# Attention beside a two-layer MLP and a routed MLP on one core: the second score product on 128 rows, and the high part of the weights cast on ScalarE throughout

## The chip, the core and the metric

The kernel runs on one core of a Trainium2 chip. The core has a matrix engine (TensorE, PE in the profile, with its weight loads as PEld), VectorE (DVE), ScalarE (ACT), GpSimd (POOL) and SyncE (SP), which here only issues transfers. Each engine works through its own instructions in the order in which the program lists them, and waits on semaphores for the others. The metric is the device time of one execution in microseconds, the median of the runs; lower is better.

## The reference

Four batches of eight heads, 576 tokens, 64 numbers a head. Queries and keys are rotated, their scores go through a softmax, and the weights multiply the values. The result, 2304 rows of 512, goes through a two-layer MLP with a leaky ReLU, and then through a second MLP whose weights are those of the best of eight experts, chosen row by row.

```python
def rotate(x):
    x1, x2 = (x[..., :half], x[..., half:])
    return np.concatenate([x1 * cos - x2 * sin, x1 * sin + x2 * cos], axis=-1)
scores = scale * np.matmul(rotate(q), rotate(k).transpose(0, 1, 3, 2))
attn = np.exp(scores - np.max(scores, axis=-1, keepdims=True))
x = np.matmul(attn / (np.sum(attn, axis=-1, keepdims=True) + 1e-09), v)
...
h = x @ w_in
y = np.maximum(0.01 * h, h) @ w_out
...
expert_idx = np.argmax(logits, axis=1)
for e in range(E):
    mask = expert_idx == e
    out[mask] = gate_w[mask, None] * (np.maximum(y[mask] @ w1[e], 0.0) @ w2[e])
```

## The kernel before, in words

**Numbers in two parts.** Queries, keys, values, weights of the softmax and rows of the MLP are each held as a high part in 16 bits and a low part (what the rounding left), so that products of 16-bit numbers add up to nearly 32-bit accuracy.

**Pairs and units.** Two heads form a pair g; there are 16 pairs. A pair has nine units: u = 0 to 7 are 128 queries of one head each, u = 8 is the last 64 queries of both heads. That makes 144 units.

**Preparing a pair** (`prep`, lines 372 to 478). The pair's queries and keys are rotated, scaled, and split into the tile `stg` [128 tokens, 5 slots, 5 blocks, 128]. Slots 0 and 1 hold the queries, one slot a head: head 0 as high | low, head 1 as low | high. Slots 2 and 3 hold each head's keys' high part twice side by side: ScalarE writes it once (line 421), VectorE copies it (line 469, 443 for the first pair). Slot 4 holds the low parts of both heads side by side. One transfer that transposes (line 474, 25 blocks of 128 by 128) turns `stg` into `stk`, where the numbers lie on the partitions: `stk[:, h]` has a head's query parts on its two halves, `stk[:, 2 + h]` the keys' high part on both halves, and `stk[:, 4]` the keys' low parts, one head a half.

**A unit's stages.** Scores (`a_scores`, line 494): for each half of the keys (288 columns) a first product over all 128 rows, line 502, gives (high + low of q) times high of k, and a second over the 64 rows of that head, line 503, adds high of q times low of k. That is four products a unit, eight for u = 8. Then the maximum on VectorE (line 510), the exponential E on ScalarE (line 515), the weights' high part (`a_hi`), their low part on VectorE (line 527), a transposing transfer of both to `PT` (line 531), the products with the values (line 548), and ScalarE's copy of the result (`xo`, line 558). `a_hi` runs on ScalarE (line 521) as long as some job that decodes the MLP's weights lives, and on VectorE (line 523) after that: 54 units and 90 units.

**The MLP's units.** A unit of the MLP is h (line 266, twelve products of 256 columns, or 24 of 128), ScalarE's scaled copy g (line 274), VectorE's leaky ReLU (line 278), ScalarE's cast gh (line 282), GpSimd's low part gl (line 286), and six products into acc (line 297). The PSUM tile that h is written to has one buffer, so the next h waits for the leaky ReLU of the last.

**What sets the order.** Everything is issued in a hand-written order (`step`, line 1002). Step i runs the exponential and the later stages of unit i - 1, the maximum of unit i, the value products of unit i - 4, the scores of unit i + 1, and at most one unit of the MLP. The stages within a step follow one of three strings; the third, once the MLP's weights are decoded, is `FESXfHsLGVKAshlC2x` (E exponential, X maximum, H the high part, L the low part and the transfer, S h, G g, K leaky ReLU, h gh, V values, C scores, 2 the products into acc). Side work (preparing pairs, finishing rows, routing, decoding weights) is cut into pieces; a piece is taken in a slot (`s`, `x`) when its step has come and the estimated budgets of the engines allow. After the last unit the rest of the MLP's units run alone, and then the experts.

Of the kernel before, what the change touches and what calls it, by code (L numbers as in the profile page):

```python
# [36 lines left out]
HI_ACT = 1  # L37
# [64 lines left out]
def attention_moe_kernel(ctx: ExitStack, tc: tile.TileContext, qkv, w_in, w_out, emb, tau, w1, w2,  # L102
# [269 lines left out]
    def prep(g):  # L372
# [37 lines left out]
        def stacks():  # L410
            stg = qkp.tile([128, 5, 5, 128], F16, name="stg")
            s2 = stg.rearrange("p s c x -> p (s c x)")
            qhi = s2[:, 0:1408].rearrange("p (h x) -> p h x", h=2)[:, :, 0:640].rearrange("p h (c x) -> p h c x", c=5)[:, :, :, 0:64]
            return (s2, qhi, stg[:, 2:4], [stg[:, 0, :, 64:128], stg[:, 1, :, 0:64]],
                    [stg[:, 4, :, 64 * h:64 * h + 64] for h in range(2)])
# [11 lines left out]
        if g == 0:  # L427
# [9 lines left out]
            s2, qhi, khd, qlo, klo = stacks()  # L437
# [3 lines left out]
            hi(khd[:, :, :, 0:64], 1)  # L441
            lo(qlo, 0, qhi)
            nc.vector.tensor_copy(out=khd[:, :, :, 64:128], in_=khd[:, :, :, 0:64])
            lo(klo, 1, khd[:, :, :, 0:64])
        else:
# [17 lines left out]
            s2, qhi, khd, qlo, klo = stacks()  # L463
            yield Piece(A=1.44)
            hi(qhi, 0)
            hi(khd[:, :, :, 0:64], 1)
            yield Piece(V=1.2)
            lo(qlo, 0, qhi)
            nc.vector.tensor_copy(out=khd[:, :, :, 64:128], in_=khd[:, :, :, 0:64])
            yield Piece(V=0.93)  # L470
            lo(klo, 1, khd[:, :, :, 0:64])
        yield Piece(at=i0 - 1)
        stk = stp.tile([128, 5, 640], F16, name="stk")
        nc.sync.dma_start_transpose(out=stk.rearrange("p s (c x) -> p (s c) x", c=5), in_=s2)
# [19 lines left out]
    def a_scores(g, u):  # L494
        stk = pairs[g][0]
        ps = psS.tile([128, 2, 512], F32, name="S")
        todo = [(u % 2, u // 2 * 128, 128, 0)] if u < 8 else [(0, 512, 64, 0), (1, 512, 64, 64)]
        for n in range(2):
            ks = slice(288 * n, 288 * n + 288)
            for h, c0, m, o in todo:  # L500
                hr = slice(64 * h, 64 * h + 64)
                nc.tensor.matmul(ps[o:o + m, n, 0:288], lhsT=stk[:, h, c0:c0 + m], rhs=stk[:, 2 + h, ks], start=True, stop=False)  # L502
                nc.tensor.matmul(ps[o:o + m, n, 0:288], lhsT=stk[hr, h, c0:c0 + m], rhs=stk[hr, 4, ks], start=False, stop=True)  # L503
        return ps
# [13 lines left out]
    def a_hi(e, i):  # L518
        p = pep.tile([128, 2 * S], F16, name="P", bufs=3)
        if i % (HI_ACT if M.unit else HI_A1) == 0 and any(z.live for z in wjobs):  # L520
# [776 lines left out]
```

## Time and profile before

| | us |
|---|---|
| median of 3 runs | 1069.04 |
| the three runs | 1068.91, 1069.04, 1073.39 |
| the profiled execution, its own time | 1070.07 |
| its span, first to last instruction | 1068.2 |
| TensorE busy, of the span | 956.1 (90%) |
| VectorE busy | 825.6 (77%) |
| ScalarE busy | 701.0 (66%) |
| GpSimd busy | 366.3 (34%) |

The span falls into four stages: up to about 183 us the MLP's weights are decoded beside the first 39 units; to about 262 us the decoding runs out while the MLP's units have begun; to 683 us the other units and the MLP's units share the step; after 683 us come the rest of the MLP and the experts. A row of the timeline has the start, the length, the engine, the line, output and inputs, and a count where like instructions are merged; in brackets stands the engine's idle time before it and what ended it. Ends of products are modelled, so the time from one product's start to the next one's start says more than a product's length.

### The profile page before, as it was taken

Reading aid. Unit: us, or ns where it says so; the run is one execution under the profiler, and the core shown is the slowest. Engines: PE = TensorE matmul, PEld = TensorE weight load, DVE = VectorE, ACT = ScalarE, POOL = GpSimd, SP = SyncE. Lnnn points to the kernel's source line nnn. Section 1 sums busy time; section 2 is a strip of 40 time slices with the busy share of each in tenths; the row PEclk is TensorE's granted clock in tenths of the full one; section 3 lists DMA queues with packets and bytes.
Section 4 is the critical chain, followed back from the end, with each engine's and each line's share of the span. In section 5 each row is a group of like instructions: output and inputs, shape, how many; then the busy total and the mean of one; then the engine's idle time right before and its main releaser. Section 6 shows DMA issues by size and latency. Waiting matters only on the chain. (4 is left out here: it accounts for less than half of the span.)

```text
span 1068.2 us, 19714 instructions
## 1 busy us (share of the span) xinstructions
PE 956.1 (90%) x6737; PEld 710.7 (67%) x6737; DVE 825.6 (77%) x1670; ACT 701.0 (66%) x1349; POOL 366.3 (34%) x414
## 2 busy tenths in 40 slices
PE   1667767888999999999999999999999899999996
PEld 1334334656666767677776677778877778888885
DVE  6999998887799764887988867313476999998992
ACT  6878878777646645556665544535345888888883
POOL 2244432534335432453444423322233362211111
PEclk9999999989999999999999999999999999999999
DMA  8988989875867873488678654201152111115190
GB/s 227 192 195 219 231 198 174 173 158 112 166 115 125 190 106 82 67 156 168 104 148 158 92 115 83 60 2 41 30 179 103 36 60 41 53 47 198 34 344 20
DMA packets 273611, 133.54 MB, mean 125 GB/s; under 512 B 244951, under 2 KB 253399, under 8 KB 273504
## 3 DMA queue, kind: packets, MB, share of 16 engines
q1 hardware_dynamic: 270304, 122.24, 52.6%
q0 software_dynamic: 3200, 9.97, 2.8%
q8 instruction: 55, 0.90, 0.3%
q14 instruction: 52, 0.43, 0.1%
HBM read 120.04 MB, written 10.49 MB: 122 GB/s over the span
## 5 line engine op out<-in xcount | busy, mean ns | idle before, releaser
L266 PE MATMUL h<-xT,wi 128*128 128x256 f16 (+1 forms) x1920 | 215.7, 264 | 20.5 <-DVE g L278 14.4
L286 POOL TENSOR_TENSOR gl<-g,gh 128x256 fp32r<-128x256 f32 x144 | 112.9, 784 | 329.7 <-ACT gh L282 304.2
L266 PEld LDWEIGHTS <-wi 128*128 128x128 f16 x1920 | 168.8, 99 | 65.0 <-issue 47.1
L297 PE MATMUL acc<-wo,gh 128*128 128x512 f32 x576 | 195.8, 421 | 0.0
L274 ACT ACTIVATE g<-h,uw 128x256 f32<-128x256 f32 (+1 forms) x160 | 70.1, 449 | 123.6 <-PE h L266 115.4
L278 DVE SCALAR_TENSOR_TENSOR g<-h,uw,g 128x256 f32<-128x256 f32 (+1 forms) x160 | 71.0, 452 | 102.4 <-ACT g L274 102.4
L282 ACT ACTIVATE gh<-g 128x256 fp32r<-128x256 f32 x144 | 60.1, 417 | 117.2 <-DVE g L278 116.5
L527 DVE SCALAR_TENSOR_TENSOR P<-E,P 128x576 f16<-128x576 f32 x144 | 119.8, 832 | 17.8 <-ACT P L521 15.4
L502 PE MATMUL S<-stk 128*128 128x288 f16 (+1 forms) x320 | 105.8, 331 | 29.1 <-ACT E L515 27.8
L548 PE MATMUL o<-v,PT 128*128 128x65 f16 (+3 forms) x1770 | 103.3, 215 | 30.1 <-ACT xo L558 14.7
L515 ACT ACTIVATE E<-S,amx,sc 128x576 f32<-128x576 f32 x144 | 117.8, 818 | 9.8 <-DVE E L510 9.5
L548 PEld LDWEIGHTS <-PT 128*128 128x128 f16 (+1 forms) x1770 | 92.3, 111 | 43.3 <-issue 25.2
L510 DVE TENSOR_SCALAR_CACHE_REDUCE E<-S,sc 128x576 f32<-128x576 f32 x144 | 116.4, 808 | 2.3 <-PE S L503 2.0
L297 PEld LDWEIGHTS acc<-wo,gh 128*128 128x128 f32 x576 | 98.2, 190 | 26.1 <-issue 0.5
L297 PE MATMUL acc<-wo,gl 128*128 128x512 f32 x288 | 114.8, 399 | 0.0
L503 PE MATMUL S<-stk 64*128 64x288 f16 (+1 forms) x320 | 106.2, 332 | 0.0
L503 PEld LDWEIGHTS <-stk 64*128 64x128 f16 (+1 forms) x320 | 31.3, 98 | 88.9 <-issue 67.8
L936 POOL DMA_INDIRECT out<-eo,idi x18 | 25.5, 1416 | 153.7 <-ACT eo L934 153.0
L390 POOL TENSOR_TENSOR t<-raw,tab 128x320 f32<-128x320 f32 x62 | 66.4, 1098 | 8.3 <-DMA raw<-in_qkv 8.3
L523 DVE TENSOR_SCALAR P<-E 128x576 f16<-128x576 f32 x90 | 52.8, 586 | 18.6 <-ACT E L515 16.9
L297 PEld LDWEIGHTS acc<-wo,gl 128*128 128x128 f32 x288 | 54.6, 190 | 13.6 <-POOL gl L286 0.9
L502 PEld LDWEIGHTS <-stk 128*128 128x128 f16 (+1 forms) x320 | 33.6, 105 | 33.6 <-issue 12.8
(237 smaller groups left out, 1883.2 us busy)
## 6 DMA issues: line engine op xcount, KB each, us to landing
rb<-in_w SPq DMA_DIRECT2D x78, 512.0 KB
ra<-in_w SPq DMA_DIRECT2D x76, 512.0 KB
raw<-in_qkv SPq DMA_DIRECT2D x15, 640.0 KB
raw<-in_w_in SPq DMA_DIRECT2D x16, 512.0 KB
raw<-in_w_out SPq DMA_DIRECT2D x16, 512.0 KB
raw<-in_qkv SPq DMA_DIRECT2D x18, 320.0 KB
x2s<-x SPq DMA_DIRECT2D x18, 256.0 KB
v<-v SPq DMA_DIRECT2D x16, 162.5 KB
```

Of the source, the lines that this page charges most:

```text
L266: nc.tensor.matmul(m.h[:, c0:c1], lhsT=wi[:, a, c, 128 * f:128 * f + 128], rhs=xT[j][:, 4 * b_ + c, 0:c1 - c0], start=(n == 0), stop=(n == ...
L274: nc.scalar.activation(out=m.g[:, c0:c1], in_=m.h[:, c0:c1], func=AF.Copy, scale=uw[:, f:f + 1])
L278: nc.vector.scalar_tensor_tensor(out=m.g[:, c0:c1], in0=m.h[:, c0:c1], scalar=uw01[:, f:f + 1], in1=m.g[:, c0:c1], op0=ALU.mult, op1=ALU.max)
L286: nc.gpsimd.tensor_tensor(out=m.gl, in0=m.g, in1=m.gh.bitcast(F32), op=ALU.subtract)
L297: nc.tensor.matmul(M.acc[t], lhsT=g_[:, tt], rhs=wo[:, a, f], start=(f == 0 and n == 0), stop=(f == NF - 1 and n == 2))
L390: eng.tensor_tensor(out=t2[t][:, :, :, o:o + 32], in0=raw[:, t, :, :, i:i + 32], in1=sn[:, :, o:o + 32].unsqueeze(1).to_broadcast([128, 2, ...
L502: nc.tensor.matmul(ps[o:o + m, n, 0:288], lhsT=stk[:, h, c0:c0 + m], rhs=stk[:, 2 + h, ks], start=True, stop=False)
L503: nc.tensor.matmul(ps[o:o + m, n, 0:288], lhsT=stk[hr, h, c0:c0 + m], rhs=stk[hr, 4, ks], start=False, stop=True)
L510: nc.vector.tensor_scalar(out=e.rearrange("p (a b) -> p a b", a=2), in0=ps[:, :, 0:288], scalar1=pairs[g][2][:, 1:2], scalar2=None, op0=AL ...
L515: nc.scalar.activation(out=e.rearrange("p (a b) -> p a b", a=2), in_=ps[:, :, 0:288], func=AF.Exp, scale=sc[:, 0:1], bias=mx)
L527: nc.vector.scalar_tensor_tensor(out=p[:, 576:1152], in0=e, scalar=P_UP, in1=p[:, 0:576], op0=ALU.mult, op1=ALU.subtract)
L548: nc.tensor.matmul(o[ob:ob + m, oc + z:oc + z + w], lhsT=pt[:, i, q0:q0 + m], rhs=v16[:, i, h, c:c + w], start=(n == 0), stop=(n == len(to ...
```

## The change

It has three edits. First, `stg` has four slots: two of queries, as before, one of the keys' high parts (both heads side by side) and one of their low parts. The key slots are transposed by themselves into a new tile `kt`, the query slots into `stk[:, 0:2]`, and four plain transfers of 64 partitions by 1280 numbers copy each head's keys, high and low, from its half of `kt` to both halves of `stk`. VectorE's copy of the high part is gone. Second, both score products of a unit run over all 128 rows: the second is now (high + low of q) times low of k, which adds the product of the two low parts. Third, `a_hi` goes to ScalarE in all 144 units. Besides, the on-chip memory set aside for descriptors of GpSimd's transfers shrinks from 16384 (the default) to 4096 bytes a partition.

```diff
         def stacks():
-            stg = qkp.tile([128, 5, 5, 128], F16, name="stg")
+            stg = qkp.tile([128, 4, 5, 128], F16, name="stg")
...
-            return (s2, qhi, stg[:, 2:4], [stg[:, 0, :, 64:128], stg[:, 1, :, 0:64]],
-                    [stg[:, 4, :, 64 * h:64 * h + 64] for h in range(2)])
+            return (s2, qhi, stg[:, 2].rearrange("p c (h x) -> p h c x", h=2), [stg[:, 0, :, 64:128], stg[:, 1, :, 0:64]],
+                    [stg[:, 3, :, 64 * h:64 * h + 64] for h in range(2)])
...
             yield Piece(A=1.44)
             hi(qhi, 0)
-            hi(khd[:, :, :, 0:64], 1)
-            yield Piece(V=1.2)
+            hi(khi, 1)
+            yield Piece(V=0.93)
+            lo(klo, 1, khi)
+            yield Piece(V=0.93)
             lo(qlo, 0, qhi)
-            nc.vector.tensor_copy(out=khd[:, :, :, 64:128], in_=khd[:, :, :, 0:64])
-            yield Piece(V=0.93)
-            lo(klo, 1, khd[:, :, :, 0:64])
+        yield Piece(at=i0 - 2)
+        kt = stp.tile([128, 2, 640], F16, name="kt", bufs=1)
+        nc.sync.dma_start_transpose(out=kt.rearrange("p s (c x) -> p (s c) x", c=5), in_=s2[:, 1280:2560])
         yield Piece(at=i0 - 1)
-        stk = stp.tile([128, 5, 640], F16, name="stk")
-        nc.sync.dma_start_transpose(out=stk.rearrange("p s (c x) -> p (s c) x", c=5), in_=s2)
+        stk = stp.tile([128, 6, 640], F16, name="stk")
+        nc.sync.dma_start_transpose(out=stk[:, 0:2].rearrange("p s (c x) -> p (s c) x", c=5), in_=s2[:, 0:1280])
+        for h in range(2):
+            for z in range(2):
+                nc.sync.dma_start(out=stk[64 * z:64 * z + 64, 2 + 2 * h:4 + 2 * h], in_=kt[64 * h:64 * h + 64])
...
-                hr = slice(64 * h, 64 * h + 64)
-                nc.tensor.matmul(ps[o:o + m, n, 0:288], lhsT=stk[:, h, c0:c0 + m], rhs=stk[:, 2 + h, ks], start=True, stop=False)
-                nc.tensor.matmul(ps[o:o + m, n, 0:288], lhsT=stk[hr, h, c0:c0 + m], rhs=stk[hr, 4, ks], start=False, stop=True)
+                for a in range(2):
+                    nc.tensor.matmul(ps[o:o + m, n, 0:288], lhsT=stk[:, h, c0:c0 + m], rhs=stk[:, 2 + 2 * h + a, ks], start=(a == 0), stop=(a == 1))
...
-        if i % (HI_ACT if M.unit else HI_A1) == 0 and any(z.live for z in wjobs):
+        if i % (HI_ACT if M.unit else HI_A1) == 0:
...
-    nc = bacc.Bacc("TRN2", target_bir_lowering=False, num_devices=1)
+    nc = bacc.Bacc("TRN2", target_bir_lowering=False, num_devices=1, dynamic_dma_scratch_size=4096)
```

On SP, around the twelfth pair (in the third stage), the kernel before has one transposing transfer between those of the units. `raw`, `v` and `PT` are the next pair's inputs, the values and the units' weights.

```order
L531 DMA_TRANSPOSE PT<-P 128x9x128 x6
L474 DMA_TRANSPOSE stk<-stg 128x25x128
L370 DMA raw_5751<-in_qkv 128x1280
L531 DMA_TRANSPOSE PT<-P 128x9x128 x2
L489 DMA v_117<-v_117 64x1040
L490 DMA v_117<-v_117 64x1300
```

The same place after the change:

```order
L535 DMA_TRANSPOSE PT<-P 128x9x128 x6
L472 DMA_TRANSPOSE kt<-stg 128x10x128
L476 DMA_TRANSPOSE stk<-stg 128x10x128
L479 DMA stk<-kt 64x1280 x4
L370 DMA raw_5850<-in_qkv 128x1280
L535 DMA_TRANSPOSE PT<-P 128x9x128 x2
```

25 blocks have become 20, in two transfers, and four copies follow that wait for the first of them to land, ahead of the units' next transfers.

On ScalarE, three steps in the third stage of the kernel before (`xo` is the copy of the values' result, `x` and `junk` are side work):

```order
L515 ACTIVATE E<-S,amx,sc 128x576
L608 ACTIVATE x_6617<-x_4634,ps 128x512
L385 ACTIVATE junk,sq_6472<-raw_6272 128x640
L274 ACTIVATE g<-h,uw 128x128 x2
L558 ACTIVATE xo<-o 128x129
L385 ACTIVATE junk,sq_6472<-raw_6272 128x640
L282 ACTIVATE gh<-g 128x256
L515 ACTIVATE E<-S,amx,sc 128x576
L385 ACTIVATE junk,sq_6472<-raw_6451 128x640
L274 ACTIVATE g<-h,uw 128x128 x2
```

The same steps after the change:

```order
L519 ACTIVATE E<-S,amx,sc 128x576
L525 ACTIVATE P<-E 128x576
L612 ACTIVATE x_6682<-x_4674,ps 128x512
L385 ACTIVATE junk,sq_6537<-raw_6363 128x640
L274 ACTIVATE g<-h,uw 128x128 x2
L562 ACTIVATE xo<-o 128x129
L385 ACTIVATE junk,sq_6537<-raw_6363 128x640
L282 ACTIVATE gh<-g 128x256
L519 ACTIVATE E<-S,amx,sc 128x576
L525 ACTIVATE P<-E 128x576
```

The cast P stands between E and the side work, ahead of g. On VectorE the place of the same steps reads, before the change:

```order
L510 TENSOR_SCALAR E,amx<-S,sc 128x576
L523 TENSOR_SCALAR P<-E 128x576
L527 SCALAR_TENSOR_TENSOR P<-E,P 128x576
L278 SCALAR_TENSOR_TENSOR g<-h,uw_80,g 128x128 x2
L604 TENSOR_SCALAR xsq<-xsq 128x1
```

and after it:

```order
L514 TENSOR_SCALAR E,amx<-S,sc 128x576
L531 SCALAR_TENSOR_TENSOR P<-E,P 128x576
L278 SCALAR_TENSOR_TENSOR g<-h,uw_80,g 128x128 x2
L608 TENSOR_SCALAR xsq<-xsq 128x1
L95 TENSOR_SCALAR pt<-xsq 128x1
```

One instruction a step has left VectorE ahead of the leaky ReLU. The order of TensorE's own instructions stays as it was except for a few single products of side work that move by a step, and each unit of the MLP stands beside the same unit of the attention as before.

## Rows read from the trace of the kernel before

**Rows 1.** Busy time by stage: PE, PEld, DVE, ACT, POOL, granted clock, DMA share, GB/s.
```profile
14.00:160.00 146.00, 95.00 (x667) 50.68 (x667) 134.23 (x297) 117.63 (x230) 56.25 (x50) 1.00 0.93 207
183.00:262.00 79.00, 68.55 (x555) 47.84 (x553) 64.80 (x143) 60.12 (x130) 32.65 (x36) 0.94 0.77 157
262.00:683.00 421.00, 409.19 (x3263) 300.70 (x3262) 330.85 (x768) 233.33 (x540) 172.11 (x232) 1.00 0.65 122
683.00:1069.00 386.00, 367.24 (x2135) 301.68 (x2134) 267.66 (x389) 260.79 (x393) 96.94 (x84) 0.99 0.25 84
```
**Rows 2.** Timeline of PE in one step of the third stage (start us, length us).
```profile
340.88 0.29 PE L502 MATMUL S<-stk 128*128 128x288 f16 x1
...
341.77 0.73 PE L297 MATMUL acc<-wo,gh 128*128 128x512 f32 x2
...
343.48 1.47 PE L266 MATMUL h<-xT,wi 128*128 128x256 f16 x12
344.78 0.57 PE L548 MATMUL o<-v,PT 128*128 128x129 f16 x9
```
**Rows 3.** The same, around the eight score products of a unit u = 8.
```profile
506.44 0.31 PE L502 MATMUL S<-stk 128*64 128x288 f16 x1
...
508.34 0.74 PE L297 MATMUL acc<-wo,gh 128*128 128x512 f32 x2
```
**Rows 4.** Groups by form, 262 to 683 us: first score products (the second ones are as many).
```profile
L502 PE MATMUL S<-stk 128*128 128x288 f16 x156 | 45.5, 292 | 2.7 <-ACT E L515 2.7
...
L502 PE MATMUL S<-stk 128*64 128x288 f16 x40 | 12.4, 310 | 0.0
```
**Rows 5.** Timeline of PE in the first stage: two neighbouring score products.
```profile
65.55 0.42 PE L502 MATMUL S<-stk 128*128 128x288 f16 x1
65.90 0.42 PE L503 MATMUL S<-stk 64*128 64x288 f16 x1
```
**Rows 6.** Groups of the whole span (busy us, mean ns): the casts and the copy.
```profile
L523 DVE TENSOR_SCALAR P<-E 128x576 f16<-128x576 f32 x90 | 52.8, 586 | 18.6 <-ACT E L515 16.9 <-DMA PT<-P 1.0
L521 ACT ACTIVATE P<-E 128x576 f16<-128x576 f32 x54 | 36.8, 681 | 7.5 <-DMA PT<-P 6.2
L469 DVE COPY stg<-stg 128x640 f16<-128x640 f16 x15 | 9.0, 602 | 0.0
```
**Rows 7.** The copy's group in the first stage alone, 14 to 160 us.
```profile
L469 DVE COPY stg<-stg 128x640 f16<-128x640 f16 x4 | 1.3, 318 | 0.0
```
**Rows 8.** Waits from 262 to 683 us: total us, times, longest us.
```profile
ACT g L274 <- PE h L266: 71.6, 53, 3.7
DVE g L278 <- ACT g L274: 40.6, 27, 3.1
...
PE h L266 <- DVE g L278: 7.3, 9, 2.0
```
**Rows 9.** Timeline of one step in which VectorE comes last, up to the next h.
```profile
345.21 0.47 ACT L274 ACTIVATE g<-h,uw 128x256 f32<-128x256 f32 x1
...
345.61 1.00 DVE L425 SCALAR_TENSOR_TENSOR stg<-raw,ps,stg 128x320 f16<-128x320 f32 x2
...
347.21 0.47 DVE L278 SCALAR_TENSOR_TENSOR g<-h,uw,g 128x256 f32<-128x256 f32 x1
...
347.73 1.47 PE L266 MATMUL h<-xT,wi 128*128 128x256 f16 x12
```
**Rows 10.** Groups of ACT from 183 to 262 us: the cast, one a unit.
```profile
L521 ACT ACTIVATE P<-E 128x576 f16<-128x576 f32 x16 | 10.8, 676 | 0.0
```
**Rows 11.** Timeline of the start: SP's transfers and the first score product.
```profile
13.55 4.48 SPq L474 DMA_TRANSPOSE stk<-stg  x1
...
18.75 0.55 SPq L489 DMA_DIRECT2D v<-v  x1
...
19.79 0.42 PE L502 MATMUL S<-stk 128*128 128x288 f16 x1 [1.24 <-DMA stk<-stg]
```
**Rows 12.** Waits of PE from 14 to 160 us: value products for the transposed weights.
```profile
PE o L548 <- DMA PT<-P: 11.9, 5, 5.2
```

More of the change, by code (lines that the diff above doesn't have):

```diff
@@ L436, in prep @@
             s3 = scales(pb)
-            s2, qhi, khd, qlo, klo = stacks()
+            s2, qhi, khi, qlo, klo = stacks()
             hi(qhi, 0)
@@ L462, in prep @@
             s3 = scales(pb)
-            s2, qhi, khd, qlo, klo = stacks()
+            s2, qhi, khi, qlo, klo = stacks()
             yield Piece(A=1.44)
             hi(qhi, 0)
-            hi(khd[:, :, :, 0:64], 1)
-            yield Piece(V=1.2)
+            hi(khi, 1)
+            yield Piece(V=0.93)
+            lo(klo, 1, khi)
+            yield Piece(V=0.93)
             lo(qlo, 0, qhi)
-            nc.vector.tensor_copy(out=khd[:, :, :, 64:128], in_=khd[:, :, :, 0:64])
-            yield Piece(V=0.93)
-            lo(klo, 1, khd[:, :, :, 0:64])
+        yield Piece(at=i0 - 2)
+        kt = stp.tile([128, 2, 640], F16, name="kt", bufs=1)
+        nc.sync.dma_start_transpose(out=kt.rearrange("p s (c x) -> p (s c) x", c=5), in_=s2[:, 1280:2560])
         yield Piece(at=i0 - 1)
-        stk = stp.tile([128, 5, 640], F16, name="stk")
-        nc.sync.dma_start_transpose(out=stk.rearrange("p s (c x) -> p (s c) x", c=5), in_=s2)
+        stk = stp.tile([128, 6, 640], F16, name="stk")
[3 more added lines that the diff above has]
+                nc.sync.dma_start(out=stk[64 * z:64 * z + 64, 2 + 2 * h:4 + 2 * h], in_=kt[64 * h:64 * h + 64])
         pairs[g] = (stk, s3, sc, v16)
```

## The prediction

> **What bounds the kernel now.** I read busy time by stage first, then the timeline of single steps, then the waits. From 262 to 683 us, where attention and the MLP share the step, PE is busy 409.2 of 421 us, VectorE 330.9, ScalarE 233.3 [rows 1]. Time taken out of PE there comes out of the end unless another engine takes its place. After 683 us no touched instruction runs. Before 183 us PE doesn't set the pace: from 14 to 160 us it is busy 95.0 of 146 us, VectorE 134.2, and the transfer engines 0.93. From 183 to 262 us nothing is full: PE 68.6, VectorE 64.8, ScalarE 60.1 of 79 us.
>
> The timeline of a step shows what PE's time is made of. Its four score products start at 340.88 and the next work at 341.77: 0.89 us, 0.223 each, for 288 columns [rows 2]. The twelve products of h, 256 columns each and each with weights of its own, take from 343.48 to 344.78, 0.108 each, or 0.423 ns a column [rows 2]. At that rate 288 columns take 0.122 us; the score products, which alternate between 128 and 64 rows, pay 0.10 us more each. In the first stage two neighbours stand 0.35 us apart [rows 5]; at half the rate 288 columns take 0.244, so again 0.11 is left over. What is left over stays the same at both rates, so it is a fixed gap at each change between 128 and 64 rows. (The window of that stage prints a granted clock of 1.00 [rows 1], but its products run at 1.2 GHz by their spacing; the step of rows 2 runs at 2.4.)
>
> **The change, part by part.**
>
> *The score products.* With 128 rows in both there is no alternation, and a unit's four products should take 4 x 0.122 = 0.49 us, 0.40 less. Not less than 0.122, since the columns must pass; not more than today's 0.223. I take 0.122, since h has the same rows and weights. A unit u = 8 takes 506.44 to 508.34, 1.90 us for eight, 0.238 each [rows 3]; these have 64-column weights and are 0.015 dearer now, which I keep: 8 x 0.137 = 1.10, 0.80 less (bounds 0 and 0.92). From 262 to 683 us there are 156 / 2 = 78 ordinary units and 40 / 4 = 10 of the others [rows 4]: 78 x 0.40 + 10 x 0.80 = 39.2 us off PE.
>
> The 64-column weights are where a rule speaks against the change. The Trainium skill, TensorEngine Tiling (Array Packing), Restrictions, says that tiling by columns disables fast weight loading, so that products with 64-column weights could stay slow; by it the sum would be 31.2 instead of 39.2. No row of this case shows such products without the change of rows, so it stays a bound.
>
> *The cast moves from VectorE to ScalarE.* 88 of the 90 casts are in this stage, so VectorE loses 88 x 0.586 = 51.6 us and ScalarE gets 88 x 0.681 = 59.9 [rows 6]. With ten copies of 0.602 gone as well, VectorE stands at 273 us, ScalarE at 293, PE at 370. ScalarE then is at 0.79 of PE; VectorE was at 0.81 before and PE still reached 97%. So the load alone doesn't put ScalarE in front.
>
> Where the cast stands matters more. It is queued ahead of g, and behind g come the leaky ReLU and the next h, whose tile has one buffer. ScalarE waits for h before g in 53 of about 88 steps, 71.6 us, 1.35 each [rows 8]: there 0.68 more fits into the wait. In the other 35 g follows other work of ScalarE, and 35 x 0.68 = 24 us is the most that this can cost. Against it stands VectorE's queue. In the step of rows 9, g ends at 345.68, but VectorE is still at the side work and the low part, and reaches the leaky ReLU at 347.21; h starts at 347.73, 0.05 after it. Such steps lose 0.586 ahead of the leaky ReLU, so they can follow the shorter PE. VectorE waits for g in only 27 steps. Waits that the profile shows as PE's own are 7.3 us. Bounds: plus 24 and minus 6 (half of the 11.8 us that PE idles in this stage); I take 5 us lost, since most rows look like the 53. Third stage: 39.2 - 5 = 34.2 us.
>
> *183 to 262 us.* There are 16 units [rows 10], at most 16 x 0.40 = 6.4 us; the cast is on ScalarE already. No engine is full, so the loop across engines sets the pace, and a shorter PE shortens only its own part of it. I take 3 us.
>
> *Up to 183 us.* VectorE loses four copies, 1.3 us [rows 7]. The transfers gain 4 x 64 x 1280 numbers of 2 bytes, 0.66 MB a pair, and lose 5 blocks of 128 x 128, 0.16 MB. At 207 GB/s [rows 1] the net 0.49 MB is 2.4 us a pair, four pairs: 0 to 10 us if transfers set the pace. VectorE, not they, is at 92%, so I take 1 us lost.
>
> *The start.* The transposing transfer of 25 blocks takes SP from 13.55 to 18.03, 0.18 a block, and the first score product starts 1.76 after it [rows 11]. Now ten blocks of keys take 1.8, ten of queries 1.8, and four copies of about 0.55 (as the transfers of `v` [rows 11]) follow the keys' landing, and have to land: 13.2 + 1.8 + 1.8 + 2.2 + 1.8 = 20.8 against 19.79. I take 1 us lost (0 to 2).
>
> *SP in the later stages.* A pair holds SP for 3.6 + 2.2 = 5.8 us plus any wait for the keys to land, against 4.5. The units' transposing transfers queue behind it. Their readers come three steps later, and a step is 343.48 to 347.73 [rows 2, 9], 4.25 us, so some 12 us are to spare and I take nothing.
>
> *The smaller descriptor memory.* It serves GpSimd's row transfers alone, after 683 us. PE idles 18.8 us there [rows 1], so 0 to 19 if all of that doubled; I take nothing, as nothing in that stage waits for it by any row that I read.
>
> **The sum** against the profiled execution's 1070.07 us: -34.2 - 3 - 1.3 + 1 + 1 = -36.5, so 1033.6. The median of the runs is 1.0 below that execution: **1032.5 us**.
>
> **The rivals.**
>
> *ScalarE becomes the bound.* g comes 0.68 us later in all 35 steps where ScalarE has no wait to fill, 24 us in place of my 5: 1032.5 + 19 = 1051.5. For it: E, cast, side work and g stand in one queue. Against it: the 1.35 us waits, and VectorE's lateness in steps like that of rows 9.
>
> *The change doesn't do what it says.* If the gap was the weights' load and not the change of rows, the products stay at 0.223, and what is left is VectorE's relief, at most the 7.3 us that PE waited for the leaky ReLU [rows 8]: 1069 - 7 + 2 = 1064. Against it: h loads weights for each product and still takes 0.108. By the Trainium skill, TensorE: Matmul & The Clock Gate, Part 3, a weight load overlaps a running product only where the row groups differ, which after the change they never do; by that rule this rival would be the forecast. The products of h already overlap their loads with equal row groups, so the trace disagrees.
>
> *The clock falls.* From 183 to 262 us the mean granted clock is 0.94: parts ran at 1.2 GHz, after PE had been waiting. PE now waits more there. If the whole stage ran at 1.2 GHz, PE's 62 us would become 62 x 0.94 / 0.5 = 117, 38 over the 79: 1032.5 + 3 + 38 = 1073.5, no change that can be measured. Against it: once PE is full again it has come back each time.
>
> *SP's queue, the slower side.* The copies wait for the keys to land while the units' transfers stand behind them. If that makes one value product in each pair wait as long as the longest such wait of the first stage, 5.2 us [rows 12], 15 pairs cost 78: 1032.5 + 78 = 1110. It decides from 37 / 15 = 2.5 us a pair on. Against it: 12 us of slack, and no such wait among PE's after 262 us.
>
> **How the numbers follow.** Forecast 0.70, ScalarE 0.15, no gain in the products 0.05, the clock 0.04, SP's queue 0.06. What a measurement tells from no change is 0.5%, 5.3 us. The first two are faster (0.85), the next two within it (0.09), the last slower (0.06). The low end takes every bound that helps: 40.4 (all products at 0.122) + 6 + 6.4 + 1.3 = 54, so 1015 from the median; 1013 with a little for the first stage. The high end takes in ScalarE's rival: 1053. That leaves the last three out.
>
> **What would show it.** Right: score products 0.12 to 0.14 apart at 2.4 GHz; PE's busy time from the first MLP unit to the last score some 40 us less and the stage about 35 shorter; the time after it unchanged; 0.68 a unit more on ScalarE. Wrong: score products still at 0.22; more of PE's time waiting on the leaky ReLU behind a late g; value products waiting for `PT`; a granted clock of 0.5 over longer stretches before 262 us.

## The result, and the profile after

The changed kernel takes **1062.02 us** (median of 5 runs, 1060.84 to 1064.22) where the kernel before took 1070.79 on the same chip: a ratio of 0.9915, with a 95% interval of 0.9900 to 0.9931. The forecast was 1032.5 (1013 to 1053). The direction was right, the size wrong by 29.5 us: three quarters of the gain are missing.

Busy time by stage after the change; the columns are those of [rows 1].

```profile
14.00:160.00 146.00, 71.33 (x646) 50.68 (x647) 127.77 (x287) 112.83 (x219) 46.48 (x46) 0.71 0.88 203
183.00:262.00 79.00, 59.61 (x561) 46.57 (x560) 63.96 (x152) 59.04 (x126) 26.94 (x31) 0.92 0.86 177
262.00:683.00 421.00, 378.60 (x3346) 307.23 (x3343) 290.67 (x689) 299.78 (x656) 180.35 (x240) 0.98 0.70 135
683.00:1058.00 375.00, 362.74 (x2109) 298.17 (x2107) 266.30 (x384) 256.99 (x384) 96.56 (x82) 1.00 0.26 86
```

In the third stage PE is busy 378.6 of 421 us and no longer 409.2 [rows 1]. PE has become faster and now waits. What it waits for has to be looked up. (The 0.71 of the first row, after 1.00, is no loss of pace: the changed kernel's score products stand 0.240 us apart at 36 us, where 1.00 is printed, and at 102 us, where 0.50 is; both are 1.2 GHz, half the pace of the products below.)

The products themselves do what was forecast, and those of a unit u = 8 more. PE's timeline of one step, and around a unit u = 8, against [rows 2, 3]:

```profile
323.62 0.65 PE L507 MATMUL S<-stk 128*128 128x288 f16 x4
324.01 0.72 PE L297 MATMUL acc<-wo,gh 128*128 128x512 f32 x2
...
334.87 0.69 PE L507 MATMUL S<-stk 128*64 128x288 f16 x8
335.49 0.73 PE L297 MATMUL acc<-wo,gh 128*128 128x512 f32 x2
```

Four products now hold PE for 0.39 us before acc starts, and held it for 0.89; the eight of a unit u = 8 for 0.62, and held it for 1.90. Within the four they start 0.122 us apart, for each column the very spacing of the products of h, and acc starts 0.03 after the fourth. So the gap belonged to the change between 128 and 64 rows; the run `wide_no_copies` below, which changes nothing but the rows, shows the same.

To compare the same work, take the 90 units from the exponential of unit 53 to that of unit 143: first the kernel before, then the changed one (columns as in [rows 1]).

```profile
260.00:668.00 408.00, 396.19 (x3156) 289.90 (x3153) 326.94 (x753) 228.48 (x529) 168.06 (x223) 1.00 0.66 124
```

```profile
265.30:662.60 397.30, 356.57 (x3162) 289.31 (x3160) 282.38 (x661) 286.62 (x626) 172.83 (x227) 0.98 0.71 138
```

PE's busy time falls by 39.6 us, its idle time rises from 11.8 to 40.7, and 10.7 us remain. Before these units the changed kernel is 5.4 us late (unit 53's exponential starts at 265.3 and started at 259.9), and after them it gains 2.3 us (400.2 to 397.9): 5.4 - 10.7 - 2.3 = -7.6, within rounding the difference of the spans (1068.2 and 1060.5).

The waits after the change, from 14 to 183 us (total us, times, longest):

```profile
PE o L552 <- DMA PT<-P: 35.6, 13, 8.3
ACT P L525 <- DMA PT<-P: 17.9, 8, 5.8
```

and from 262 to 683 us, against [rows 8]:

```profile
DVE P L531 <- ACT P L525: 64.2, 51, 5.1
ACT g L274 <- PE h L266: 24.8, 28, 1.7
PE h L266 <- DVE g L278: 18.6, 19, 2.8
ACT P L525 <- DMA PT<-P: 18.6, 5, 5.2
PE o L552 <- DMA PT<-P: 10.4, 5, 2.6
```

Two things are new. ScalarE waits for PE in 28 steps and no longer in 53 [rows 8], while PE waits for VectorE's leaky ReLU 18.6 us, 7.3 before. And transposing transfers (`PT`) come late, for the value products and for ScalarE's cast. How one late transfer travels is seen from 288 to 304 us, in the timeline of SP, PE, ScalarE and VectorE:

```profile
288.59 1.43 SPq L472 DMA_TRANSPOSE kt<-stg  x1
290.06 1.57 SPq L476 DMA_TRANSPOSE stk<-stg  x1
292.23 2.39 SPq L479 DMA_DIRECT2D stk<-kt  x4
...
295.87 4.84 SPq L535 DMA_TRANSPOSE PT<-P  x2
...
303.31 0.60 PE L552 MATMUL o<-v,PT 128*128 128x65 f16 x14 [2.65 <-DMA PT<-P]
303.35 0.68 ACT L525 ACTIVATE P<-E 128x576 f16<-128x576 f32 x1 [5.23 <-DMA PT<-P]
...
304.07 0.76 DVE L531 SCALAR_TENSOR_TENSOR P<-E,P 128x576 f16<-128x576 f32 x1 [5.13 <-ACT P L525]
```

SP works on the pair from 288.59 to 294.62, and the units' transposing transfers of this time start at 295.87. A value product on PE waits 2.65 us for one of them. ScalarE, which wants to *write* a P buffer that such a transfer still has to read, stands still for 5.23 us, with the copies of h and the next exponential in its queue. PE's granted clock answers:

```profile
300.00:304.00 4.00, 1.35 (x24) 0.99 (x22) 0.00 (x0) 0.65 (x2) 0.00 (x0) 1.00 1.37 170
304.00:308.00 4.00, 3.17 (x20) 2.18 (x18) 2.65 (x5) 3.05 (x8) 2.25 (x3) 0.53 1.11 241
308.00:312.00 4.00, 4.00 (x28) 3.10 (x26) 3.40 (x7) 3.65 (x8) 3.78 (x5) 0.62 0.52 103
```

After PE was busy for only 1.35 of 4 us it runs at 0.53 of full speed, that is at 1.2 GHz nearly throughout, and comes back to 2.4 GHz within the third row.

### The profile page after: what moved, and what is told of

Its sections match the earlier page's. It is cut to its first block, busy times and chain, and to the rows that moved or that the text cites. A ratio compares the mean times of both kernels' runs of the same rounds, so it can differ in the third digit from the quotient of the medians.

```text
span 1060.5 us, 19876 instructions
## 1 busy us (share of the span) xinstructions
PE 882.0 (83%) x6737; PEld 709.4 (67%) x6737; DVE 773.9 (73%) x1564; ACT 755.8 (71%) x1439; POOL 360.6 (34%) x414
## 5 line engine op out<-in xcount | busy, mean ns | idle before, releaser
L266 PE MATMUL h<-xT,wi 128*128 128x256 f16 (+1 forms) x1920 | 218.2, 265 | 36.9 <-DVE g L278 31.2
L286 POOL TENSOR_TENSOR gl<-g,gh 128x256 fp32r<-128x256 f32 x144 | 110.7, 769 | 317.2 <-ACT gh L282 293.5
L531 DVE SCALAR_TENSOR_TENSOR P<-E,P 128x576 f16<-128x576 f32 x144 | 127.6, 886 | 92.7 <-ACT P L525 91.8
L507 PE MATMUL S<-stk 128*128 128x288 f16 (+1 forms) x640 | 115.4, 332 | 36.4 <-ACT E L519 34.5
L525 ACT ACTIVATE P<-E 128x576 f16<-128x576 f32 x144 | 98.2, 682 | 40.1 <-DMA PT<-P 36.5
L297 PEld LDWEIGHTS acc<-wo,gh 128*128 128x128 f32 x576 | 100.9, 193 | 18.6 <-issue 2.5
L507 PEld LDWEIGHTS <-stk 128*128 128x128 f16 (+1 forms) x640 | 58.1, 112 | 54.2 <-issue 39.2
L390 POOL TENSOR_TENSOR t<-raw,tab 128x320 f32<-128x320 f32 x62 | 63.5, 1054 | 13.2 <-DMA raw<-in_qkv 10.1
L587 POOL TENSOR_TENSOR x<-xo,rd 128x128 f32<-128x128 f32 (+1 forms) x33 | 20.9, 632 | 102.7 <-DVE rd L579 80.3
L929 PE MATMUL h<-w,hth 128*128 128x512 f32 x176 | 55.4, 396 | 0.4 <-ACT hth L913 0.4
```

Of the source, the lines that this page charges most:

```text
L266: nc.tensor.matmul(m.h[:, c0:c1], lhsT=wi[:, a, c, 128 * f:128 * f + 128], rhs=xT[j][:, 4 * b_ + c, 0:c1 - c0], start=(n == 0), stop=(n == ...
L286: nc.gpsimd.tensor_tensor(out=m.gl, in0=m.g, in1=m.gh.bitcast(F32), op=ALU.subtract)
L297: nc.tensor.matmul(M.acc[t], lhsT=g_[:, tt], rhs=wo[:, a, f], start=(f == 0 and n == 0), stop=(f == NF - 1 and n == 2))
L525: nc.scalar.activation(out=p[:, 0:576], in_=e, func=AF.Copy, scale=P_UP)
L531: nc.vector.scalar_tensor_tensor(out=p[:, 576:1152], in0=e, scalar=P_UP, in1=p[:, 0:576], op0=ALU.mult, op1=ALU.subtract)
L929: nc.tensor.matmul(OP[kk], lhsT=h_[:, c, :], rhs=wt[a][c // 2][:, 512 * (c % 2):512 * (c % 2) + 512], start=(n == 0), stop=(n == len(todo) ...
```

## The experiments

The kernel before took 1070.7 to 1071.7 us beside them (medians); each ratio is to the runs on the same chip. Times at single units come from one profiled execution of each kernel. Runs with the new transfers, with added copies, or with four buffers for P also have the smaller descriptor memory, which by itself is worth about 2 us at the very end (see Small steps).

### The parts apart

**The cast alone**, in the kernel before.

```diff
-        if i % (HI_ACT if M.unit else HI_A1) == 0 and any(z.live for z in wjobs):
+        if i % (HI_ACT if M.unit else HI_A1) == 0:
```

> The kernel before with the cast on ScalarE to the end and nothing else. Theory A: PE's work is as it was, g comes 0.68 us later in a third of the steps, so 1070 to 1090 us and more of VectorE's time waiting for ScalarE's cast (91.8 us in the changed kernel). Theories B and C: VectorE's relief counts, 1063 to 1070 us.

Measured: 1064.11 us, ratio 0.9934 (0.9915 to 0.9952). **The changed kernel with the cast taken back** to VectorE (the same line the other way round):

> The changed kernel, but the cast goes back to VectorE once the decoding is over; wide products, keys' copies and the smaller descriptor memory stay. Theory A (the cast in ScalarE's queue ahead of g, the MLP's scaled copy, eats the gain): most of the 35 us that were missing from the forecast come back, about 1035 us. Theory B (the new transfers eat it, through value products that wait for the transposed weights): about as the changed kernel, 1060 us, and those waits stay at 40 us or more. Theory C (the fallen clock eats it): as B, with the clock's falls still there.

Measured: 1072.30, ratio 1.0006 (0.9989 to 1.0023). So the cast on ScalarE gains 7 us in the kernel before and 10 in the changed one, where none of the three theories had it gain anything. It is no cost.

**The new tiles and transfers alone**, with the second product on 64 rows and the cast as before:

```diff
-                for a in range(2):
-                    nc.tensor.matmul(ps[o:o + m, n, 0:288], lhsT=stk[:, h, c0:c0 + m], rhs=stk[:, 2 + 2 * h + a, ks], start=(a == 0), stop=(a == 1))
+                hr = slice(64 * h, 64 * h + 64)
+                nc.tensor.matmul(ps[o:o + m, n, 0:288], lhsT=stk[:, h, c0:c0 + m], rhs=stk[:, 2 + 2 * h, ks], start=True, stop=False)
+                nc.tensor.matmul(ps[o:o + m, n, 0:288], lhsT=stk[hr, h, c0:c0 + m], rhs=stk[hr, 3 + 2 * h, ks], start=False, stop=True)
```

> The changed kernel's tiles and transfers (keys transposed by themselves, four copies a pair), but the second score product on the head's 64 rows as before, and the cast on VectorE as before. Theory A: the transfers are hidden, 1065 to 1075 us. Theory B: 1085 us or more, with value products waiting for the transposed weights some 30 us longer than before's 12. Theory C: about 1070, and no falls of the clock after 262 us, since PE is as full as before.

Measured: 1084.73, ratio 1.0129 (1.0097 to 1.0161). The preparation, with its new order of pieces, costs 13.5 us by itself.

**The products on 128 rows without a transfer more.** In the kernel before the low parts' slot already holds one head's low part on each half, so the second product may run over all of it. It then adds (low of q) times (low of the other head's k), a term of the size of the rounding squared.

```diff
-                nc.tensor.matmul(ps[o:o + m, n, 0:288], lhsT=stk[hr, h, c0:c0 + m], rhs=stk[hr, 4, ks], start=False, stop=True)
+                nc.tensor.matmul(ps[o:o + m, n, 0:288], lhsT=stk[:, h, c0:c0 + m], rhs=stk[:, 4, ks], start=False, stop=True)
```

> The kernel before, transfers and cast unchanged, with one edit: the second score product runs over all 128 rows of both operands, so that it adds the head's low part of q times the other head's low part of k, a term that the reference doesn't have. PE's relief alone. Theory A: 1030 to 1040 us. Theory B: the same. Theory C: the clock falls as often as in the changed kernel, since PE has the same gaps, and the time is 1050 us or more.

Measured: 1048.95, ratio 0.9794 (0.9764 to 0.9824): 22 us gained, 9 less than theories A and B had at least, and without C's falls of the clock (granted 1.00 in the row below). **With the cast on ScalarE throughout as well:**

> wide_no_copies (both products on 128 rows, transfers as before; the second product adds low of q times the other head's low of k, which the reference doesn't have) plus the cast on ScalarE to the end. If the two gains are independent: 1049 - 7 = 1042 us. If the shorter PE is what needs VectorE's relief (the loop h, g, leaky ReLU): more than 7, 1035 to 1040. If the cast now stands in the way of g: 1047 to 1052.

Measured: 1043.22, ratio 0.9741 (0.9722 to 0.9759). The two edits that were meant to gain give 28 us together; the preparation takes 19 of them back. The same 90 units in the first of the two kernels, and in the second:

```profile
259.40:646.40 387.00, 349.48 (x3157) 285.35 (x3155) 326.23 (x753) 227.89 (x530) 170.35 (x223) 1.00 0.72 131
```

```profile
258.60:640.80 382.20, 350.39 (x3157) 284.98 (x3154) 283.46 (x666) 283.40 (x619) 167.68 (x223) 1.00 0.72 132
```

The products take 46 us off PE's busy time (396.2 to 349.5 and 350.4). Its idle time rises from 11.8 to 37.5 with the cast on VectorE, and to 31.8 with the cast on ScalarE. So 26 of the 46 us, then 20, come back as waiting, with no transfer added. The largest part is one wait, from 262 to 683 us, in the first kernel and in the second; it was 7.3 [rows 8], so it makes 20 of the 26 us and 12 of the 20:

```profile
PE h L266 <- DVE g L278: 27.7, 26, 3.2
```

```profile
PE h L266 <- DVE g L278: 18.9, 22, 2.6
```

### The order of the preparation's pieces

The diff also moves pieces, which the list of its three edits leaves out: the keys' low part stands ahead of the queries', and one more piece stands ahead of the transposing transfer. **This order alone, in the kernel before:**

```diff
-            yield Piece(V=1.2)
-            lo(qlo, 0, qhi)
+            yield Piece(V=0.93)
             nc.vector.tensor_copy(out=khd[:, :, :, 64:128], in_=khd[:, :, :, 0:64])
-            yield Piece(V=0.93)
             lo(klo, 1, khd[:, :, :, 0:64])
+            yield Piece(V=0.93)
+            lo(qlo, 0, qhi)
+        yield Piece(at=i0 - 2)
```

> The kernel before with only the preparation's pieces cut as in the changed kernel (low part of k ahead of that of q, other budgets, one more piece), so that the side work stands in the changed kernel's order; transfers, copy, products and cast as before. If the order of the side work costs the 13 us of transfers_alone: 1080 us or more. If the transfers cost them: 1069 to 1073 us.

Measured: 1078.62, ratio 1.0067 (1.0048 to 1.0087), between the two theories. **The same in the kernel with 128 rows, the cast and no copies:**

> The kernel before with the second product over 128 rows of the low parts' slot and the cast on ScalarE throughout (1043.2 us), with the changed kernel's order of the preparation's pieces (low part of the keys ahead of that of the queries, one more piece ahead of the transposing transfer); one transposing transfer a pair, no copies. In the kernel before this order alone cost 7.4 us. If it costs as much here, 1049 to 1052, and the copies with their two transposing transfers cost some 11 of the 19 us. If it costs nothing here, as in the changed kernel itself, which with the old order took 1064.5, 1042 to 1045.

Measured: 1049.10, ratio 0.9792 (0.9773 to 0.9811), 5.9 us more than without. **The new transfers with the old order of pieces**, first with the products and the cast of before, then in the changed kernel:

> transfers_alone with the pieces cut as before the change (both transposing transfers and the four copies issued where the one transfer was). If the transfers cost the 13 us: 1080 to 1086 us. If the order does: 1069 to 1073 us, with value products waiting about 12 us for the transposed weights up to 183 us, as before, in place of 25.

Measured: 1089.07, ratio 1.0174 (1.0151 to 1.0196).

> The changed kernel (wide products, copies, cast on ScalarE) with the pieces cut as before the change. If the transfers cost the gain: about 1062 us. If the order does: 1040 to 1048 us, and the falls of the clock after 270 us mostly gone.

Measured: 1064.48, ratio 0.9938 (0.9919 to 0.9958). All in one table, in us:

| products and cast | transfers | old order | new order |
|---|---|---|---|
| before | before | 1071.2 | 1078.6 |
| before | new | 1089.1 | 1084.7 |
| 128 rows, ScalarE | before | 1043.2 | 1049.1 |
| 128 rows, ScalarE | new | 1064.5 | 1062.0 |

The transfers cost 18 to 21 us in the old order, 6 to 13 in the new one. The new order costs 6 to 7 us by itself and gives 2 to 4 back where the transfers are new. Neither price can be had from the other. In the last row the preparation as a whole costs 18.8 us: 5.9 for the order, and then 12.9 for the transfers. The rows with new transfers hold the 2 us that the smaller descriptor memory gives at the end, so up to the last unit the transfers cost about 2 us more than these differences.

Where the order costs shows in a step of the changed kernel (VectorE, then PE):

```profile
365.86 1.16 DVE L425 SCALAR_TENSOR_TENSOR stg<-raw,ps,stg 128x320 f16<-128x320 f32 x2
366.94 0.75 DVE L531 SCALAR_TENSOR_TENSOR P<-E,P 128x576 f16<-128x576 f32 x1
367.61 0.47 DVE L278 SCALAR_TENSOR_TENSOR g<-h,uw,g 128x256 f32<-128x256 f32 x1
...
368.14 1.85 PE L266 MATMUL h<-xT,wi 128*128 128x256 f16 x12 [2.10 <-DVE g L278]
```

The queries' low part stands on VectorE ahead of the leaky ReLU, and so do, since 362.16, the keys' low part and the next rows of the MLP's result (line 308, 363.78). PE waits 2.10 us, and the granted clock of the next 3.9 us is 0.62. The kernel without copies has the same step with the new order, and there PE waits 2.17 us. With the old order both low parts fall into one step as well (338.43 and 340.86 in that kernel), but one without the MLP's rows, and PE waits only 0.68 us, for a small instruction behind the leaky ReLU. So it matters which step a piece falls into. The other places weren't traced to single rows; over the 90 units the order adds 3.8 us of idle time and 3.6 of busy time to PE.

### What of the transfers costs

**Copies that nobody reads**, added to the kernel before with the smaller descriptor memory (from the pair before, so without a wait); then the same copies reading `stk` that has just been transposed, so that SP waits for it to land:

```diff
+        if g:
+            dup = stp.tile([128, 4, 640], F16, name="dup", bufs=1)
+            for h in range(2):
+                for z in range(2):
+                    nc.sync.dma_start(out=dup[64 * z:64 * z + 64, 2 * h:2 * h + 2], in_=pairs[g - 1][0][64 * h:64 * h + 64, 0:2])
```

> The kernel before plus, for each pair from the second on, four plain transfers of 64 x 1280 numbers on SP behind the transposing one, from the pair before's stk into a tile that nobody reads: the bytes and the issue of the new copies without a wait for a landing (and the smaller descriptor memory). Theory B1 (SP's hold for the wait on the keys' landing delays the units' transposing transfers): 1069 to 1075 us. Theory B2 (bytes and issue in front of them do): 1083 us or more.

> The same four copies, but from the stk that the transposing transfer before them has just written, so that SP waits for its landing. B1: 1083 us or more, and at least 8 us above copies_added. B2: as copies_added, within 4 us.

Measured: 1095.50, ratio 1.0257 (1.0217 to 1.0297), and 1118.75, ratio 1.0465 (1.0422 to 1.0507). Behind a transposing transfer of 25 blocks the copies cost 24.8 us, and the wait for the landing 23.2 more, so each theory has half of the price; SP's own wait there is 30.6 us in all:

```profile
SPq L479 <- DMA stk<-stg: 30.6, 15, 3.0
```

In the changed kernel the copies wait for ten blocks only, with the other ten issued in between:

```profile
SPq L479 <- DMA kt<-stg: 11.3, 14, 2.3
```

**The changed kernel with half the bytes in four copies, and with copies that needn't wait:**

```diff
-        for h in range(2):
+        for a in range(2):
             for z in range(2):
-                nc.sync.dma_start(out=stk[64 * z:64 * z + 64, 2 + 2 * h:4 + 2 * h], in_=kt[64 * h:64 * h + 64])
+                nc.sync.dma_start(out=stk[64 * z:64 * z + 64, 2 + a], in_=kt[0:64, a])
```

> The changed kernel with four copies a pair as before, each of 64 partitions by 640 numbers in place of 1280; both heads read the first head's keys, so the second head's scores are wrong. Number of transfers and SP's wait for the keys stay. The changed kernel took 1062.0 us, the kernel with the same products and cast and no copies 1043.2. If the bytes of the copies set their price, about half of the 19 us comes back: 1051 to 1055. If the wait for the landing or the number of transfers sets it, 1059 to 1062.

```diff
-                nc.sync.dma_start(out=stk[64 * z:64 * z + 64, 2 + 2 * h:4 + 2 * h], in_=kt[64 * h:64 * h + 64])
+                nc.sync.dma_start(out=stk[64 * z:64 * z + 64, 2 + 2 * h:4 + 2 * h], in_=kts[max(g - 1, 0)][64 * h:64 * h + 64])
```

> The changed kernel, but the copies read the keys of the pair before, which landed long ago (a second buffer for them); so the scores of all pairs but the first are wrong, and SP doesn't wait ahead of the copies. Bytes and number of transfers stay. With copies that nobody reads the wait made 23 of 48 us. If the wait for the landing sets the price here too, about half of the 19 us comes back: 1050 to 1055. If the bytes set it: 1059 to 1063. The experts chosen may differ, so the start of the last unit's exponential (662.6 us in the changed kernel) is the better measure: some 10 us earlier by the first theory, 3 at most by the second.

Measured: 1059.82, ratio 0.9892 (0.9860 to 0.9923), and 1059.43, ratio 0.9880 (0.9851 to 0.9908). Each gives back 2 to 3 us, with an interval that overlaps that of the changed kernel. By the start of the last unit's exponential, the measure named beforehand for the second, it is 2.3 and 1.2 us (660.3 and 661.4, after 662.6). Neither theory got its 10 us: the bytes by themselves are not the price, and the large price of the landing in the kernel before is not the price here.

**Two transposing transfers in place of one**, without copies:

```diff
-        nc.sync.dma_start_transpose(out=stk.rearrange("p s (c x) -> p (s c) x", c=5), in_=s2)
+        nc.sync.dma_start_transpose(out=stk[:, 2:5].rearrange("p s (c x) -> p (s c) x", c=5), in_=s2[:, 1280:3200])
+        nc.sync.dma_start_transpose(out=stk[:, 0:2].rearrange("p s (c x) -> p (s c) x", c=5), in_=s2[:, 0:1280])
```

> The same kernel without copies and in the old order, with a pair's keys (15 blocks) and queries (10) transposed by two transfers in place of one of 25. If a further transposing transfer a pair on SP's queue has a price of its own, 1046 to 1051. If only what stands behind the copies counts, 1042 to 1044.

Measured: 1042.97, ratio 0.9730 (0.9709 to 0.9751), as without the split.

**The copies issued by GpSimd** (`nc.gpsimd.dma_start` in line 479):

> The changed kernel with the four copies issued by GpSimd in place of SP: the same bytes, and SP is not held. If SP's hold is what costs: 1043 to 1052 us. If the bytes on the transfer engines cost: 1060 us or more. If GpSimd's own queue (gl, the finished rows) is held instead: 1065 us or more with longer waits on gl.

Measured: 1084.55, ratio 1.0123 (1.0102 to 1.0144), 22.5 us worse. SP doesn't wait any more, but GpSimd does, and over the whole run PE waits for late transfers as long as before:

```profile
POOL stk L479 <- DMA kt<-stg: 77.8, 15, 11.3
PE o L552 <- DMA PT<-P: 50.1, 16, 10.6
```

The Trainium skill, DMA: Bandwidth & Descriptors, Issuing engines are not separate DMA queues, says that transfers of all issuing engines share the same 16 DMA engines. The 50.1 us, against 46.0 with SP as the issuer, agree. But in the 90 units alone that wait falls from 10.4 to 5.2 us and ScalarE's for `PT` from 18.6 to 10.4, while the products into acc wait 14.5 us for GpSimd's gl, which they didn't with SP as the issuer. That fits four issues ahead on SP's queue making transfers late there, but it doesn't show it: the units are slower in this run (411.0 us for the 90), which gives the transfers more time, and GpSimd's own waits hide what it is worth.

### The buffers

**Four buffers for P in place of three**, in the changed kernel; then two for the MLP's rows `x16` besides; then four for P where there are no copies (with the smaller descriptor memory, for room):

```diff
-        p = pep.tile([128, 2 * S], F16, name="P", bufs=3)
+        p = pep.tile([128, 2 * S], F16, name="P", bufs=4)
```

> The changed kernel with four buffers for the weights P in place of three. If late transposing transfers stall ScalarE through P's buffers (36.5 us of ScalarE's waits in the changed kernel): ScalarE's cast waits under 10 us for them, and 1048 to 1055 us. If they do harm through the value products that read PT: 1060 us, and the cast's waits become longer waits of those products (46 us now).

> The changed kernel with four buffers in place of three for the weights P and two in place of one for x16, the MLP's rows. With four buffers of P alone it took 1054.7 us. If ScalarE's wait for x16 behind late transfers (4 to 5 us of its waits) sits on the path, 1050 to 1052. If it is hidden, or the rest of the price stands in other places (value products that wait for PT, 45 us of PE's waits in that run), 1054 to 1056.

> The kernel before with its second product over all 128 rows of the low parts' slot and the cast on ScalarE throughout, no copies (1043.2 us), with four buffers in place of three for P and the smaller descriptor memory that makes room for it. If late transfers stall ScalarE through P only because of the copies, no change: 1042 to 1044. If three buffers of P cost something without copies as well, 1036 to 1041; the 7.4 us that the fourth buffer gave back in the changed kernel are the most.

Measured: 1054.67, ratio 0.9850 (0.9834 to 0.9867); 1052.12, ratio 0.9817 (0.9792 to 0.9842); and **1036.57**, ratio 0.9674 (0.9650 to 0.9698), 25.5 us faster than the changed kernel and the fastest of all. The cast's group on ScalarE in the changed kernel, and with four buffers (busy us, mean ns, idle before it):

```profile
L525 ACT ACTIVATE P<-E 128x576 f16<-128x576 f32 x144 | 98.2, 682 | 40.1 <-DMA PT<-P 36.5
```

```profile
L525 ACT ACTIVATE P<-E 128x576 f16<-128x576 f32 x144 | 98.3, 683 | 4.0
```

The fourth buffer removes the whole wait of ScalarE, 36.5 us, and the kernel gains 7.3. Without copies it seems to gain 6.6 too, but 2 of these are the smaller descriptor memory's, which that kernel has with four buffers and not with three. Up to the last unit's exponential the fourth buffer gives 7.6 us with the copies (662.6 to 655.0) and 3.5 without (640.8 to 637.3). So the stall through P, which the row at 303.35 shows so plainly, is real and stands for about 4 of the 21.8 us between the two kernels up to there; 17.7 remain with four buffers.

## Why the prediction was wrong

By stretches: up to unit 53's exponential 2.3 us of gain were forecast (3 and 1.3, less 1 and 1) and 5.4 were lost; in the 90 units 34.2 were forecast and 10.7 gained; behind them nothing was forecast and 2.3 were gained. The 23.5 us missing from the 90 units divide by the runs into 8.4 for the products and the cast (25.8 in place of 34.2), 7.4 for the order of the pieces and 7.7 for the transfers.

**The products: right, and too small.** Forecast were 39.2 us off PE, 0.49 us a unit and 1.10 for u = 8. Measured are 0.39 and 0.62, and 46 us over the 90 units. The bound "not less than 0.122" held for the ordinary units; the products of a unit u = 8 take 0.078 each. The rival that the gap was the weights' load is refuted: 288 columns pass every 0.122 us, each product with weights of its own. The Trainium skill, TensorE: Matmul & The Clock Gate, Part 3, says that a load overlaps a running product only where the row groups differ; it also names a background weight buffer as a way to be ahead, and only that agrees with these rows. The bound taken from the Trainium skill, TensorEngine Tiling (Array Packing), Restrictions, that 64-column weights could stay slow, didn't come true either: these gained most.

**"I take 5 us lost": the first wrong step.** It put the cost of the loop on the cast, and took it from the waits of a kernel in which PE was last. Once PE is faster, the loop from h over g and the leaky ReLU back to h is last in many more steps: PE's idle time rises by 20 us without any new transfer, 26 with the cast on VectorE. The cast on ScalarE has the opposite sign: it shortens that wait (27.7 to 18.9) and gains 6 to 10 us. In the units 54 to 143 the products and the cast gave 408.0 - 382.2 = 25.8 us in place of 34.2. The rival "ScalarE becomes the bound" falls with it. From unit 36 to 53 the run without copies gave 1.7 us (forecast 3), the changed kernel 2.8.

**The order of the pieces: a step that was missing.** The prediction showed VectorE's order at one place and priced no move. By itself the order costs 5.9 us (7.4 in the 90 units, and a little gained before them); the step at 366 us is one place of it.

**"Some 12 us are to spare and I take nothing", "1 us lost": the largest error.** The copies and their transposing transfers cost 12.9 us in place of 2. Against the run with the new order and no copies, 7.3 us lie before unit 53 (its exponential starts at 265.3 and not at 258.0; 1.9 of that stand already at the first unit's, 28.7 and not 26.8) and 7.7 in the 90 units (397.3 and not 389.6). That makes 15.0; the 2.1 between it and the 12.9 come back at the very end. The slack was counted for the readers of `PT` alone, and of a single transfer; the row at 292.23 and those behind it show four at a time, and a writer that waits as well. In the 90 units PE waits 10.4 us for `PT`; without the new transfers, in the new order, it is next to nothing (262 to 683 us):

```profile
PE o L548 <- DMA PT<-P: 0.9, 1, 0.9
```

For the stretch up to 183 us the prediction said that VectorE, at 92%, and not the transfers set the pace; [rows 1] have the transfers at 0.93. But bytes were not the price either: half of the copies' bytes gave 2.2 us in the whole kernel. PE's waits for `PT` up to 183 us don't measure this price: they are 35.6 us here, but 32.5 with the new order and no copies. The rival "SP's queue" had the mechanism, at 78 us for 15 pairs; its 12.9 are 0.9 a pair, under the 2.5 from which it decides.

**The clock: a rival that came a little, elsewhere.** From 183 to 262 us nothing changed (0.92 after 0.94). But in the 90 units the granted clock is 0.98 and was 1.00, and PE's busy time is 356.6 us with the copies and 350.4 without; 3.6 of these 6.2 us come with the order of the pieces alone (354.0). In the changed kernel the clock falls to 1.2 GHz at 304.2, 341.8, 369.1 and 471.5 us, three times behind a wait for `PT` (2.65, 2.60 and 2.12 us) and once behind one for the leaky ReLU (2.10).

**Small steps.** The start was forecast 1 us later, with the first score product at 20.8; it stands at 21.29 and stood at 19.79 [rows 11]. Behind the last unit nothing was forecast, and 2.3 us were gained. Some 2.1 of these come from the smaller descriptor memory, which the prediction priced at nothing. The longest of GpSimd's last instructions, a DRAIN, takes 3.33 us before and 1.62 after (shortest/median/longest of three, in ns):

```profile
L1293 POOLq DRAIN  x3: 40/107/3332, 1064.1 to 1067.9; - x3
```

```profile
L1297 POOLq DRAIN  x3: 40/107/1617, 1058.1 to 1060.2; - x3
```

The instruction ahead of it (INC_SWDGE_SEM) takes 0.98 and 0.56. All seven kernels with the default memory have the longer times and take 399.9 to 400.3 us from unit 143's exponential to the end; the thirteen with the smaller one have shorter ones and take 397.3 to 398.9. Two of these, `copies_added` and the kernel without copies but with four buffers for P, share no other edit.

**What stays open** is how the transfers' price divides. Halving the bytes gives 2.2, the landing 2.6, two `x16` buffers on top of four for P 2.5, each within its uncertainty; bytes and landing weren't taken away together. A transposing transfer more costs nothing where there are no copies. The candidates left are the issue of four more transfers ahead of the units' own and the falls of the clock. The one run that takes the four issues off SP and keeps the bytes has GpSimd's waits in their place, so what they cost isn't shown.

## What to carry to other kernels

Before paying transfers to fill the rows of a product, look at what already lies in the empty ones: here the other head's low parts gave the same 128 rows without a transfer, in a kernel 19 us faster. When an engine that is last gets faster, look for the loop that comes next and count on half of the gain until a run has shown it; here 20 of 46 us came back as waiting, 12 of them in one loop. And price a transfer by all that is queued behind it, readers and writers of buffers alike, and a moved piece of side work by the one instruction behind it that closes the loop. A part of a change that is priced at nothing still needs its own run, or it hides in the price of another: here 2 us of descriptor memory in the price of the transfers.

## What was not expected of the hardware

The eight products of a unit u = 8 have 64-column weights, and four go to each half of the output. They start in pairs, 7 ns apart within a pair: eight of 288 columns take 0.62 us, where eight with 128-column weights would take 8 x 0.122 = 0.98. That the two of a pair belong to different halves is likely, but the trace doesn't name the half. The Trainium skill, TensorE: Matmul & The Clock Gate, Part 3, gives about 4 ns between such products on different tiles; the trace agrees roughly. With alternating rows, before, the same eight took 1.90 us, 0.238 apart; in `wide_no_copies`, where only the rows change, they stand in pairs as well, so the change of rows had kept them apart. The Trainium skill, TensorEngine Tiling (Array Packing), Key Properties, says that a change of the tiling mode drains the engine; that agrees with the gap of some 0.10 us at every change of rows, at 2.4 GHz [rows 2] and at 1.2 GHz [rows 5] alike.
